# Attention and a gated layer in one kernel: the seven-product layer of two token blocks begun one tile sooner, less attention work between half-width steps, one fetch sooner

## The chip, the cores and the metric

The kernel runs on one core of a Trainium2 chip. The metric is the device time of one execution in microseconds (us), the median of three runs of the same program. TensorE (PE in the rows) multiplies matrices into PSUM banks, VectorE (DVE) and ScalarE (ACT) work element by element and empty the banks, GpSimd (POOL) does element work between SBUF tiles, SyncE (SP) issues DMAs. Each engine runs its own queue strictly in order.

## The reference

```python
def _attn_ref(q, k, v):               # (8, 8, 576, 64): batch, heads, sequence, head size
    # chunks of 64 along the sequence: S = Q K^T / 8 within a chunk
    scores = scores - np.max(scores, axis=-1, keepdims=True)
    attn = np.exp(scores)
    attn = attn / (np.sum(attn, axis=-1, keepdims=True) + 1e-09)
    out = np.matmul(attn, v_c)
def _moe_ref(x, w_gate, w_val, w_out):  # x: 4608 x 512, widths 512 -> 1536 -> 512
    gate = 1.0 / (1.0 + np.exp(-(x @ w_gate)))
    return (gate * (x @ w_val) @ w_out)
```

The attention's output is reordered to 4608 tokens of 512 numbers and goes through the gated layer. All is float32.

## The kernel before, in words

The 4608 tokens are nine blocks of 512, the hidden width is twelve slices f of 128. A float32 product is made of three passes over rounded halves (high and low part of each operand), so an operand is first *split*: ScalarE casts the high part, VectorE subtracts it to get the low part. Block 0 is worked plainly at the start. Blocks 1 and 2 share one hidden tile per slice (`hidden_kept`, line 297): for each block and slice TensorE makes a gate tile and a value tile (12 matmuls each, line 278), ScalarE takes the sigmoid (line 303), VectorE multiplies (line 305). A gate-and-value pair is called a tile step here; it takes two of the four `acc` banks. The first four slices of block 1 are done in two half-width parts a and b (256 tokens); the part b steps stand in `LEAD`.

The product with `w_out` is done for two blocks at once by a seven-product scheme (`down_begin`, `down_products`): 42 *small steps* q of 12 matmuls each (line 661), every one with its own split (lines 636 and 637). `down_begin` issues the first two weight loads and the splits of q = 0, 1 and 2; in `down_products` the split of q + 3 is issued just before the matmuls of q. The pairs of blocks 3 to 8 then use the same scheme for the first product too (`first`, `middle`, `last`, line 504).

The attention of later blocks is woven in. `flow` yields it piece by piece: score products on TensorE (line 173) into two `psa` banks, two VectorE transposes out of them (738), a maximum (742) whose 32-partition halves are exchanged by four ScalarE copies (721), a subtraction (746, 747), an exponential (749, which needs another function table than the sigmoid, so a table load stands ahead of each change), the value products of the unit before (244) into the same two banks and their copies out (264 and 265, or 261), a sum (765), exchanged again, the division (769, 772, 773) and two transposes (777). A number that `flow` yields is a price in credit; `tick(share)` grants credit, so `SHARES` sets how much is issued after each step. "S" and "A" are places where TensorE's products may be inserted. After the last unit of a pair, `operands` makes the seven operands of the pair's first product: a difference on VectorE (481), a cast on ScalarE (485), the low part on VectorE (494).

The order written is the order issued on TensorE, VectorE, SyncE and GpSimd, and on ScalarE as far as blocks 1 and 2 are concerned. GpSimd meanwhile forms sums of weight quarters, writes them to DRAM, and fetches the next quarters (`keep_sums`, `fetch`); the first fetch for the pairs' second half is issued by SyncE (line 376).

Of the kernel before, what the change touches and what calls it, by code (L numbers as in the profile page):

```python
# [19 lines left out]
NF = 12  # L20
# [29 lines left out]
SHARES = {1: 1.4, 2: 1.3, "up": 1.0, "turned": 0.36}  # L50
# [3 lines left out]
def chunk_attn_moe(ctx: ExitStack, tc: tile.TileContext, q, k, v, w, out, turned_out):  # L54
# [288 lines left out]
    def keep_given(p, which):  # L343

        if p < RESIDENT:
            t = given[p, which] = dp.tile([P, 3, 2, 256], F32, name=f"given{p}{which}")
            for n, (f, k) in enumerate(((2 * p, 0), (2 * p, 1), (2 * p + 1, 1))):
                nc.sync.dma_start(t[:, n], wt[f, which][:, :, k * 256:(k + 1) * 256].bitcast(F32))
        else:
            t = whole[p, which] = dp.tile([P, 2, 2, 4, P], F32, name=f"whole{p}{which}")  # L350
            for n in range(2):
                src = wt[2 * p + n, which].bitcast(F32).rearrange("p a (k m) -> p (a k) m", k=2)
                for c in range(2):
                    nc.sync.dma_start(t[:, n, c], src[:, :, c * P:(c + 1) * P])
# [240 lines left out]
    def down_sums(n, f):  # L595

        if n < 0:
            if f in (0, 4, 6):
                t = wp.tile([P, 4, TB], F32, tag=f"u{f // 2 - f // 4}", name="t12")
                for e in range(4):  # L600
                    k = e + (0, 4, 8)[f // 2 - f // 4]
                    (t1 if k < 6 else t2)[k % 6] = t[:, e]
        elif f == 0:
            t = xp.tile([P, 8, TB], F32, tag="x", name="t1")
            for e in range(8):
                t1[e] = t[:, e]
        elif f == 6:
            both = sb.tile([P, 4, TB], F32, tag="a_both", name="t2")
            t2.update({0: t1[6], 1: t1[7], **{2 + e: both[:, e] for e in range(4)}})
        e = f % 6  # L610
        b11, b12 = (hid[n, e][:, b] for b in range(2))
        if f < 6:
            nc.vector.tensor_tensor(out=t1[e], in0=b12, in1=b11, op=ALU.subtract)
        else:
            b22 = hid[n, f][:, 1]
            nc.vector.tensor_tensor(out=t2[e], in0=b22, in1=t1[e], op=ALU.subtract)
            nc.vector.tensor_tensor(out=b12, in0=b22, in1=b12, op=ALU.subtract)
# [22 lines left out]
    def down_begin(n):  # L640

        ring["splits"], *ring["weights"] = rotation
        rotation[:] = rotation[4:] + rotation[1:4] + rotation[:1]
        for i in range(2):
            load_down(n, i)
        for q in range(3 if n < LAST else 6):
            down_split(n, q)
# [136 lines left out]
    def advance():  # L784
        now["unit"] += 2 * (now["item"] == "A")
        now["item"] = next(ahead, None)
        now["since"] = now["ticks"]

    def tick(share):
        now["ticks"] += 1  # L790
        now["credit"] += share
        while now["item"] is not None:
            if isinstance(now["item"], float):
                if now["credit"] < now["item"] / 2:
                    return
                now["credit"] -= now["item"]
            elif not (now["item"] == "wait" and now["ticks"] > now["since"] + 1
                      or now["item"] == "next" and now["ticks"] > now["since"]
                      or now["item"][0] in ("open", "freed") and now["item"][1] <= now[now["item"][0]]):
                break  # L800
            advance()
        now["credit"] = min(now["credit"], share)

    def insert(upto=4 * NB, pieces=0):


        if now["item"] == "S" or (
                now["item"] == "A" and now["unit"] < upto and now["ticks"] >= now["since"] + pieces):
            advance()

    def due(n):

        while now["item"] is not None and len([x for x in xc if x[0] == n]) < 7:
            advance()
# [4 lines left out]
    def step(m, f, span, aside=False):  # L819
        if m:  # L820
            hidden_kept(m, f, spans[span], aside)
        else:
            pending.append(hidden(m, f, spans[span]))
# [4 lines left out]
    def run(op):  # L828
        what, arg = op[0], op[1:]
        if what == "L":  # L830
            load(int(arg))
        elif what == "V":
            load_values(int(arg))
        elif what in "Ss":
            scores(int(arg), what == "s")
        elif what == "E":
            softmax(int(arg))
        elif what in "Tt":
            transposes(int(arg), what == "t")
        elif what == "A":  # L840
            values(int(arg), pairs.pop(int(arg) // 2)["pt"])
        elif what == "W":
            load_weights(int(arg[:-1]), arg[-1])
        elif what == "C":
            f, part = arg.split(".")
            convert_weights(int(f), int(part))
        elif what == "G":
            for which in range(2):
                keep_given(int(arg), which)
        elif what == "K":  # L850
            keep_outer(int(arg))
        elif what == "H":
            m, f = arg.split(".")
            step(int(m), int(f.rstrip("ab")), f.lstrip("0123456789"))
        else:
            finish()
# [5 lines left out]
    def keep(n=1):  # L862
        for _ in range(n):
            if kept:
                keep_sums(*kept.pop(0))
# [5 lines left out]
    def singles():  # L871
        for op in LEAD.split():
            run(op)
            if op[0] == "H":
                tick(SHARES[1])
                insert(12, 1)
        for m in range(1, FIRST_PAIR):
            upto = 4 * (m + 2) if m == 1 else 4 * (m + 3)
            while now["unit"] < 4 * (m + 1):
                advance()  # L880
            for f in range(FIRST_STEP if m == 1 else 0, NF):
                if m == 2 and f == 7:
                    now["open"] = 0
                if m == 2 and f == NF - 1:
                    down_begin(-1)
                step(m, f, "", True)
                tick(SHARES[m])
                insert(upto, 1)
                if m == 2 and f < NF - 2:
                    down_sums(-1, f)  # L890
                tick(SHARES[m])
                insert(upto, 1)
                if givens:
                    keep_given(*givens.pop(0))
                if kept[0][2] is None:
                    keep()

    def pair(n):
        m0 = FIRST_PAIR + 2 * n
        upto = 4 * (m0 + 4)  # L900
        order = [(p, which) for p in range(6) for which in range(2)]
        if n >= 0:
            due(n)
        for i, (p, which) in enumerate(order if n >= 0 else ()):
            if i + 1 < len(order) and i > 0:
                load_group(n, *order[i + 1])
            first(n, p, which)
            tick(SHARES["up"])
            if i:
                keep(2)  # L910
                last(n, *order[i - 1])
                tick(SHARES["up"] if i < 11 else 0)
                insert(upto, 1)
                if i > 1:
                    down_sums(n, i - 2)
            middle(n, p, which)
            tick(SHARES["up"] if i < 11 else 0)
            insert(upto, 1)
        if n >= 0:
            down_begin(n)  # L920
            last(n, *order[-1])
        now["open"] = n + 1

        def between(q):
            now["freed"] = q if n < 0 else 99
            if n < LAST:
                if q in (32, 36):
                    load_group(n + 1, 0, 0, ((q - 32) // 4,))
                if n < 0 and q == 32:
                    fetch(*kept[0], nc.sync)  # L930
                tick(SHARES["turned"] if q > 3 else 0)
                insert(upto, 1)

        down_products(n, between)
        if n < LAST:
            load_group(n + 1, 0, 1)
# [42 lines left out]
```

## Time and profile before

| | |
|---|---|
| median of 3 runs | 906.49 us (904.53 to 906.89) |
| the profiled execution | 904.59 us, span 902.8 us |
| TensorE busy | 869.1 us, 96% of the span |
| VectorE, ScalarE, GpSimd busy | 674.6, 397.4, 244.4 us |
| DMA | 216.53 MB, 240 GB/s on average |

The span runs from the first to the last instruction of the core. The first 60 us bring in weights and hold most of TensorE's idle time. Blocks 1 and 2 lie from about 169 to 298 us, their seven-product layer from 298 to 360 us, and the three pairs of blocks follow. In a row of the timeline, the first number is the start, the second the length of the stretch, and what stands in square brackets is the idle time just before it and who ended it.

### The profile page before, as it was taken

The numbers are of one execution on the slowest core, as the hardware profiler recorded it, in microseconds if no ns is written. First come the engines' busy times: TensorE is split into PE (matmuls) and PEld (weight loads), VectorE is DVE, ScalarE is ACT, GpSimd is POOL, SyncE is SP. The second block draws the span as 40 slices with busy tenths as digits, with TensorE's granted clock in tenths as the row PEclk, the third lists the DMA queues.
The fourth block names the chain that finished last, engine by engine and source line by source line (L and its number), as shares of the span: only waits on it lengthen the run. The fifth ranks groups of instructions, "written<-read, shape, count | busy, mean of one in ns | idle before, by whom it ended". The sixth has DMA issues, their size and how long they took to land.

```text
span 902.8 us, 15594 instructions
## 1 busy us (share of the span) xinstructions
PE 869.1 (96%) x6016; PEld 711.7 (79%) x6016; DVE 674.6 (75%) x1007; ACT 397.4 (44%) x734; POOL 244.4 (27%) x275
## 2 busy tenths in 40 slices
PE   4799999999999899999999999999999999999998
PEld 3678879888877687887887888888878888888886
DVE  6998955476878778787987895877778945555973
ACT  6988743334444644234326551442345511122540
POOL 0111217999994002888940000000000000000000
PEclk7999999999999999999999999999999999999999
DMA  8885586599775666999986678595565785564772
GB/s 314 292 268 197 162 282 234 204 332 374 262 252 184 210 203 234 362 328 360 351 290 196 200 237 271 194 298 168 187 190 181 225 280 198 181 202 154 232 211 94
DMA packets 152107, 216.53 MB, mean 240 GB/s; under 512 B 9056, under 2 KB 90464, under 8 KB 150496
## 3 DMA queue, kind: packets, MB, share of 16 engines
q1 hardware_dynamic: 143248, 178.29, 61.2%
q0 software_dynamic: 8784, 37.23, 11.0%
q8 instruction: 48, 0.79, 0.3%
q14 instruction: 27, 0.22, 0.1%
HBM read 169.87 MB, written 45.61 MB: 239 GB/s over the span
## 4 chain that ended last, share of the span: by engine, by line
PE 63%; DMA 1%; DVE 1%; ACT 1%; issue 1%; SPq 0%; ACTq 0%; DVEq 0%
PE dx L661 17%; PE cy L504 16%; PE cz L504 11%; PE cx L504 10%; PE dz L661 7%; DMA wr<-sums 1%; PE av L244 1%; PE sc L173 1%; DVE hx L637 0%; ACT hx L636 0%; SPq L144 0%; DVE raw L481 0%; ACT xc L485 0%; DVE hid L685 0%; ACT hs L636 0%
## 5 line engine op out<-in xcount | busy, mean ns | idle before, releaser
L504 PE MATMUL cy<-xc,wr 128*128 128x512 f32 x648 | 159.4, 390 | 1.8 <-DMA wr<-sums 1.8
L504 PEld LDWEIGHTS cy<-xc,wr 128*128 128x128 f32 x648 | 121.3, 188 | 28.2 <-DVE mx L742 2.2
L278 PE MATMUL acc<-xt,w 128*128 128x512 f32 x480 | 112.6, 392 | 0.0
L504 PE MATMUL cz<-xc,wr 128*128 128x512 f32 x432 | 107.2, 392 | 0.0
L504 PE MATMUL cx<-xc,wr 128*128 128x512 f32 x432 | 106.0, 391 | 0.0
L661 PE MATMUL dx<-hs,wd 128*128 128x512 f32 x432 | 102.1, 390 | 2.9 <-ACT hs L636 2.7
L278 PEld LDWEIGHTS acc<-xt,w 128*128 128x128 f32 x480 | 89.1, 188 | 18.9
L278 PE MATMUL g<-xt,w 128*128 128x256 f32 (+1 forms) x528 | 94.7, 335 | 7.0 <-ACT hf L287 2.6
L661 PEld LDWEIGHTS dx<-hs,wd 128*128 128x128 f32 x432 | 81.0, 188 | 20.5 <-ACT hs L636 3.1
L278 PEld LDWEIGHTS g<-xt,w 128*128 128x128 f32 x528 | 80.0, 190 | 18.9 <-ACT hf L287 3.7
L504 PEld LDWEIGHTS cx<-xc,wr 128*128 128x128 f32 x432 | 80.6, 188 | 17.3 <-DMA wr<-given 0.4
L504 PEld LDWEIGHTS cz<-xc,wr 128*128 128x128 f32 x432 | 80.3, 188 | 16.9
L661 PE MATMUL dx<-hx,wd 128*128 128x512 f32 x288 | 71.1, 393 | 1.1 <-DVE hx L637 0.7
L661 PEld LDWEIGHTS dx<-hx,wd 128*128 128x128 f32 x288 | 53.7, 188 | 14.6 <-DVE hx L637 2.2
L522 DVE TENSOR_TENSOR s<-cy,s 128x512 f32<-128x512 f32 x36 | 24.9, 690 | 51.4 <-PE cy L504 44.8
L520 ACT COPY s<-cx 128x512 f32<-128x512 f32 x36 | 21.2, 589 | 83.8 <-PE cx L504 83.7
L636 ACT CAST hs<-hid 128x512 fp32r<-128x512 f32 x66 | 38.3, 620 | 43.7 <-PE dx L661 26.5
L637 DVE TENSOR_TENSOR hs<-hid,hs 128x512 fp32r<-128x512 f32 x66 | 43.6, 703 | 13.8 <-ACT hs L636 13.8
L661 PE MATMUL dz<-hs,wd 128*128 128x512 f32 x216 | 51.2, 389 | 0.0
L359 POOL DMA_DIRECT2D outer<-w x24 | 18.8, 782 | 117.2 <-issue 49.0
L544 ACT ACTIVATE hid<-cx 128x512 f32<-128x512 f32 x18 | 10.8, 598 | 83.3 <-PE cx L504 83.3
L661 PEld LDWEIGHTS dz<-hs,wd 128*128 128x128 f32 x216 | 40.5, 188 | 8.4
(135 smaller groups left out, 1424.0 us busy)
## 6 DMA issues: line engine op xcount, KB each, us to landing
wr<-sums SPq DMA_DIRECT2D x72, 512.0 KB, 6.1
w_raw<-w_in SPq DMA_DIRECT2D x36, 512.0 KB, 5.3
wd<-outer SPq DMA_DIRECT2D x72, 256.0 KB, 5.3
wd<-outer_sums SPq DMA_DIRECT2D x16, 1024.0 KB, 6.1
wr<-whole SPq DMA_DIRECT2D x54, 256.0 KB, 4.4
qt<-q_in SPq DMA_DIRECT2D x36, 256.0 KB, 4.6
kt<-k_in SPq DMA_DIRECT2D x36, 256.0 KB, 5.0
vt<-v_in SPq DMA_DIRECT2D x36, 256.0 KB, 4.4
```

The source lines that it names most:

```text
L173: nc.tensor.matmul(sc[i][half * D:(half + 1) * D, n0:n0 + D], lhsT=x[rows, a, chunk], rhs=y[rows, a, chunk], start=True, stop=True)
L244: nc.tensor.matmul(av[c][a * D:(a + 1) * D, n0:n0 + D], lhsT=vt[u][rows, i, a, t, :], rhs=pt[rows, i, u, t, a, :], start=True, stop=True)
L278: nc.tensor.matmul(ps[:, tok], lhsT=wt[f, which][:, wpart, c:c + P], rhs=xt[m][:, part, 2 * u + i, tok], start=n == 0, stop=n == 11)
L359: nc.gpsimd.dma_start(outer[:, f, c], src[:, :, c])
L504: nc.tensor.matmul(bank, lhsT=lhs(wpart, c), rhs=x[:, part, c], start=start and k == 0, stop=stop and k == 5, skip_group_check=True)
L520: nc.scalar.copy(s1, x)
L522: nc.vector.tensor_tensor(out=u2, in0=y, in1=s1, op=ALU.add)
L544: nc.scalar.activation(hid[n, f][:, 0], x, AF.Sigmoid)
L636: nc.scalar.copy(hi, src)
L637: nc.vector.tensor_tensor(out=lo, in0=src, in1=hi.bitcast(F32), op=ALU.subtract)
L661: nc.tensor.matmul(bank[to][c], lhsT=down_lhs(r, f, wpart, c), rhs=down_in[q][part], start=r in (1, 6, 5) and (f, i) == (0, 0), stop=stop ...
```

## The change

Three numbers differ. In `singles`, a step in `LEAD` (half width) grants 1.0 of credit to the attention instead of 1.4. `down_begin` for blocks 1 and 2 is called ahead of the tile step of slice 10 of block 2 instead of slice 11. SyncE's fetch for GpSimd is issued after small step 28 instead of 32.

```diff
             if op[0] == "H":
-                tick(SHARES[1])
+                tick(SHARES["up"])
                 insert(12, 1)
...
-                if m == 2 and f == NF - 1:
+                if m == 2 and f == NF - 2:
                     down_begin(-1)
                 step(m, f, "", True)
...
-                if n < 0 and q == 32:
+                if n < 0 and q == 28:
                     fetch(*kept[0], nc.sync)
```

Since credit moves on from step to step, the first number shifts the attention of blocks 1 and 2 against the tile steps throughout. On ScalarE, at the half-width steps of slices 2 and 3, the order before was as follows (`g` is a gate product at half width, `mx` and `other` belong to the attention's maximum, `acc` is a full tile):

```order
L303 ACTIVATE hid<-g_1829 128x256
L721 COPY other<-mx_1859 32x32 x4
L303 ACTIVATE hid<-g_1866 128x256
L749 ACT_TABLE_LOAD
L749 ACTIVATE pr<-pr 128x1024
L303 ACT_TABLE_LOAD
L303 ACTIVATE hid<-g_1897 128x256
```

It is now:

```order
L303 ACTIVATE hid<-g_1829 128x256
L303 ACTIVATE hid<-g_1859 128x256
L721 COPY other<-mx_1887 32x32 x4
L303 ACTIVATE hid<-g_1894 128x256
L749 ACT_TABLE_LOAD
L749 ACTIVATE pr<-pr 128x1024
L303 ACT_TABLE_LOAD
```

The sigmoid of slice 2 has moved ahead of the exchange, that of slice 3 ahead of the exponential. On VectorE the first full tiles and the division of the same unit stood so before (`hid<-acc` is the product of a tile step, `sums` belongs to the division, `pt` to its transposes, `sc` is the next unit's score bank):

```order
L305 TENSOR_TENSOR hid<-acc,hid 128x512
L765 TENSOR_REDUCE sums_1954<-pr 128x32
L769 SCALAR_TENSOR_TENSOR sums_1954<-sums_1954,other 128x32
L772 RECIPROCAL sums_1954<-sums_1954 128x32
L773 TENSOR_TENSOR pr<-pr,sums_1954 128x1024
L777 STREAM_TRANSPOSE pt<-pr 128x512 x2
L305 TENSOR_TENSOR hid<-acc,hid 128x512
L738 STREAM_TRANSPOSE pr<-sc 128x512 x2
L742 TENSOR_REDUCE mx_2058<-pr 128x32
L305 TENSOR_TENSOR hid<-acc,hid 128x512
L746 TENSOR_TENSOR mx_2058<-mx_2058,other 128x32
```

And now:

```order
L305 TENSOR_TENSOR hid<-acc,hid 128x512
L765 TENSOR_REDUCE sums_1954<-pr 128x32
L305 TENSOR_TENSOR hid<-acc,hid 128x512
L769 SCALAR_TENSOR_TENSOR sums_1954<-sums_1954,other 128x32
L772 RECIPROCAL sums_1954<-sums_1954 128x32
L773 TENSOR_TENSOR pr<-pr,sums_1954 128x1024
L777 STREAM_TRANSPOSE pt<-pr 128x512 x2
L738 STREAM_TRANSPOSE pr<-sc 128x512 x2
L305 TENSOR_TENSOR hid<-acc,hid 128x512
L742 TENSOR_REDUCE mx_2104<-pr 128x32
L746 TENSOR_TENSOR mx_2104<-mx_2104,other 128x32
```

The product of the tile step now stands between the sum and the division, and no longer between the maximum and its use. This order comes back in every later unit of blocks 1 and 2. On TensorE the score products and the value products stand one tile step later.

At the end of block 2, ScalarE had this order (`hs` and `hx` are splits of the seven-product layer, `raw` the last value products' copies, `xc` the operands of the next pair):

```order
L749 ACTIVATE pr<-pr 128x1024
L261 COPY raw<-av 128x4x2x64 x2
L303 ACT_TABLE_LOAD
L303 ACTIVATE hid<-acc 128x512
L485 CAST xc<-raw 128x1024 x3
L636 CAST hs<-hid 128x512 x2
L636 CAST hx<-hid 128x512
L303 ACTIVATE hid<-acc 128x512
L485 CAST xc<-raw 128x1024
L636 CAST hx<-hid 128x512
```

It is now:

```order
L749 ACTIVATE pr<-pr 128x1024
L636 CAST hs<-hid 128x512 x2
L636 CAST hx<-hid 128x512
L303 ACT_TABLE_LOAD
L303 ACTIVATE hid<-acc 128x512
L261 COPY raw<-av 128x4x2x64 x2
L485 CAST xc<-raw 128x1024 x3
L303 ACTIVATE hid<-acc 128x512
L485 CAST xc<-raw 128x1024
L636 CAST hx<-hid 128x512
```

The first three splits have moved ahead of the last values' copies and of the operand casts; the fourth split still comes behind the fourth operand cast. On SyncE the fetch into `again` has moved ahead of one pair of stores, one load of layer weights and the two loads of the next pair's first group, right behind the weight load of small step 28.

## Rows read from the trace of the kernel before

**Rows 1.** The stretch of blocks 1 and 2 in the view of busy times by stretch: start and end, length, busy time and number of instructions by engine, TensorE's clock, DMA share, GB/s.

```profile
150.00:300.00 150.00, 143.40 (x1496) 118.75 (x1496) 104.91 (x119) 59.87 (x115) 121.37 (x113) 1.00 0.80 273
```

**Rows 2.** The waits of TensorE over the whole span: who waited for whom, us in total, times, longest.

```profile
PE dx L661 <- ACT hs L636: 2.7, 1, 2.7
PE cy L504 <- DMA wr<-sums: 1.8, 1, 1.8
PE g L278 <- ACT hid L303: 1.5, 1, 1.5
...
PE sc L173 <- ACT raw L261: 1.4, 3, 1.1
```

**Rows 3.** Timeline of TensorE at the half-width steps, and at the end of block 2 and the start of its seven-product layer.

```profile
165.92 3.14 PE L278 MATMUL g<-xt,w 128*128 128x256 f32 x24 [1.52 <-ACT hid L303]
168.90 5.63 PE L278 MATMUL acc<-xt,w 128*128 128x512 f32 x24
...
286.47 11.17 PE L278 MATMUL acc<-xt,w 128*128 128x512 f32 x48
300.35 0.49 PE L661 MATMUL dx<-hs,wd 128*128 128x512 f32 x1 [2.71 <-ACT hs L636]
```

**Rows 4.** Timeline of ScalarE at the half-width steps.

```profile
164.56 0.89 ACT L721 COPY other<-mx 32x32 f32<-32x32 f32 x4 [4.06 <-DVE mx L742]
165.48 0.38 ACT L303 ACTIVATE hid<-g 128x256 f32<-128x256 f32 x1
```

**Rows 5.** Timeline of VectorE at the first full tiles: the start of the division of one unit, the product behind it, the transposes of the next.

```profile
177.46 0.68 DVE L769 SCALAR_TENSOR_TENSOR sums<-sums,other 128x32 f32<-128x32 f32 x1 [1.02 <-ACT other L721]
...
181.73 0.69 DVE L305 TENSOR_TENSOR hid<-acc,hid 128x512 f32<-128x512 f32 x1 [0.42 <-issue]
182.34 1.30 DVE L738 STREAM_TRANSPOSE pr<-sc 128x512 f32<-128x512 f32 x2
```

**Rows 6.** Timeline of VectorE in block 2, two units: the products that waited for ScalarE, and one division.

```profile
246.75 0.69 DVE L305 TENSOR_TENSOR hid<-acc,hid 128x512 f32<-128x512 f32 x1 [1.64 <-ACT hid L303]
253.84 0.69 DVE L305 TENSOR_TENSOR hid<-acc,hid 128x512 f32<-128x512 f32 x1 [2.84 <-ACT hid L303]
267.69 0.69 DVE L305 TENSOR_TENSOR hid<-acc,hid 128x512 f32<-128x512 f32 x1 [1.64 <-ACT hid L303]
273.74 0.69 DVE L305 TENSOR_TENSOR hid<-acc,hid 128x512 f32<-128x512 f32 x1 [0.61 <-ACT hid L303]
278.08 2.38 DVE L769 SCALAR_TENSOR_TENSOR sums<-sums,other 128x32 f32<-128x32 f32 x1
```

**Rows 7.** Timeline of ScalarE from the last exponential of block 2's stretch to the fourth split.

```profile
291.27 1.06 ACT L749 ACTIVATE pr<-pr 128x1024 f32<-128x1024 f32 x1 [0.81 <-DVE pr L747]
292.23 1.05 ACT L261 COPY raw<-av 128x512 f32<-128x512 f32 x2
293.30 1.28 ACT L303 ACT_TABLE_LOAD   x1
294.60 0.60 ACT L303 ACTIVATE hid<-acc 128x512 f32<-128x512 f32 x1
295.09 1.99 ACT L485 CAST xc<-raw 128x1024 fp32r<-128x1024 f32 x2
...
299.68 1.13 ACT L636 CAST hs<-hid 128x512 fp32r<-128x512 f32 x2
...
304.94 0.62 ACT L636 CAST hx<-hid 128x512 fp32r<-128x512 f32 x1
```

**Rows 8.** Timeline of VectorE there: the first low part of an operand, and the first difference.

```profile
296.17 1.23 DVE L494 TENSOR_TENSOR xc<-raw,xc 128x1024 fp32r<-128x1024 f32 x1 [0.24 <-ACT xc L485]
297.43 1.22 DVE L481 TENSOR_TENSOR raw<-raw 128x1024 f32<-128x1024 f32 x1
```

**Rows 9.** Groups of VectorE's instructions by line and shape: busy us, mean ns of one, idle before. The first two rows are of the stretch 176 to 280 us, the third of 494 to 640 us.

```profile
L305 DVE TENSOR_TENSOR hid<-acc,hid 128x512 f32<-128x512 f32 x15 | 10.2, 681 | 15.8 <-ACT hid L303 13.4 <-PE acc L278 1.9 <-issue 0.4
L617 DVE TENSOR_TENSOR hid<-hid 128x512 f32<-128x512 f32 x2 | 3.3, 1638 | 0.0
...
L617 DVE TENSOR_TENSOR hid<-hid 128x512 f32<-128x512 f32 x3 | 2.0, 683 | 0.0
```

**Rows 10.** Timeline of SyncE (the weight load of small step 28, and the fetch) and of GpSimd (the first instruction that needs the fetched tile).

```profile
335.05 1.25 SPq L586 DMA_DIRECT2D wd<-outer_sums  x1
...
347.76 0.62 SPq L376 DMA_DIRECT2D again<-whole  x1
...
355.64 2.17 POOL L420 TENSOR_TENSOR a_both<-again 128x256 f32<-128x256 f32 x2 [23.09 <-DMA again<-whole]
```

**Rows 11.** Timeline of VectorE (splits of small steps 36 to 41 around the start of GpSimd's work) and of TensorE at small step 39.

```profile
349.31 1.29 DVE L637 TENSOR_TENSOR hs<-hid,hs 128x512 fp32r<-128x512 f32 x2 [0.61 <-ACT hs L636]
...
355.38 0.69 DVE L637 TENSOR_TENSOR hx<-hid,hx 128x512 fp32r<-128x512 f32 x1 [1.69 <-ACT hx L636]
355.99 2.37 DVE L637 TENSOR_TENSOR hs<-hid,hs 128x512 fp32r<-128x512 f32 x2
...
356.13 1.41 PE L661 MATMUL dz<-hx,wd 128*128 128x512 f32 x5 [0.23 <-DVE hx L637]
```

## The prediction

> **What bounds the kernel now.** I read the busy times first. TensorE is busy 96% of the span, and what it lacks lies mostly in the first 60 us, which the change leaves alone. In the stretch of blocks 1 and 2 it is busy 143.4 of 150 us [rows 1], so some 6.6 us are to be had there. The view of waits names them [rows 2]: 1.5 us once for a sigmoid at the half-width steps, 1.4 us in three pieces where score products wait for ScalarE to empty the banks, and 2.7 us at the first small step of the seven-product layer, which waits for its split. Elsewhere only the 1.8 us on a weight load stands out.
>
> Then I asked who is late. TensorE may run ahead of VectorE by two tile steps, since a step takes two of four banks. In block 2 VectorE's products of the tile steps wait for ScalarE, not for TensorE: 1.64 and 2.84 us, then 1.64 and 0.61 us [rows 6]. So from there on it is the chain between VectorE and ScalarE, which hand work to and fro, that ends last; TensorE meets it at the banks and at the splits. That makes the question: when does that chain bring the fourth split, at 305.56 us before (304.94 + 0.62) [rows 7]? Behind it no small step waits until the 0.23 us at 356.13 [rows 11].
>
> **The half-width steps.** Before, the sigmoid of slice 2 stood behind four copies that begin at 164.56, and TensorE lost 1.52 us up to 165.92 [rows 3, 4]. In the new order it stands ahead of them, and those 1.52 us go. The first full tile starts at 168.90 - 1.52 = 167.4. This shortens the whole only if TensorE's arrival sets the end of the stretch. By the step above it doesn't, so it counts zero in the sum and comes back in a rival.
>
> **What the shifted order does to the chain.** First unit: before, the division ran from 177.46 to 181.31 (181.73 less 0.42 idle), 3.85 us, then the product, then the transposes at 182.34 [rows 5]. Now the product of the second full tile stands ahead of the division. That tile ends at 167.4 + 11.2 for two tile steps [rows 3], at 178.6; product 0.69, division 3.85, a handoff of 0.1: the transposes start at 183.2, 0.85 later than before, with the same work done.
>
> Later units: the waits inside one unit change places. After the sum, the next product needs the copies and a sigmoid on ScalarE: 0.90 + 0.60 [rows 4, 7], with 0.15 for the handoffs 1.65 us, nothing of VectorE's between. After the subtraction it needs exponential, table load and sigmoid: 1.06 + 1.28 + 0.60 [rows 7], with handoffs 3.1 us, again with nothing between, because the differences for the seven products (lines 613, 616 and 617) now stand ahead of the subtraction, where they cover the copies. Together 4.75 us. Before, the same places cost 1.64 + 2.84 = 4.48 in the one unit, and 1.64 + 0.61 = 2.25 in the other [rows 6], where two long differences lay beneath the exponential. So the first kind gains nothing and loses 0.25, the second loses 2.5. Of that some 2.2 come back: the division of that unit, whose first instruction took 2.38 us beside GpSimd at 278.08 [rows 6], slips past the end of GpSimd's work. I take +0.3 for this unit and +0.2 for each of the four others, 1.1 in all.
>
> Line 617, two SBUF inputs, takes 1638 ns while GpSimd works and 683 ns where it doesn't (the page's slices show it idle there); line 305, with one input from PSUM, takes 681 beside GpSimd [rows 9]. The Trainium skill (GPSIMD Engine Reference, Specifications) says that GpSimd shares its SBUF interfaces with VectorE, with contention for instructions with two SBUF inputs. The trace agrees on who is slowed, not that each one is: by the rule all five such instructions on the path of small step 39 (below) would pay, and the sum would be 912.4 instead of 910.7; by the rows a part of them does.
>
> **Beginning the layer one tile sooner.** The first three splits now follow the exponential at once; those of q = 1 and 2 are ready in time. The fourth is not moved: it still stands behind the fourth operand cast, and that cast behind the last value products, which are now one tile step later. From the end of the exponential (292.33) to 305.56 it took 13.23 us before [rows 7]. Now, in order: three splits 1.75, table 1.28, sigmoid 0.60, two copies 1.05, first cast 1.00 [rows 7]; on VectorE the low part 1.23 and the difference 1.22 [rows 8]; third cast 1.00, sigmoid 0.60, product 0.69, low part 1.23, difference 1.22, fourth cast 1.00, split 0.62. Sum 14.5, so +1.3. TensorE then waits little at the first small step and 5 to 6 us at the fourth. The move by itself is worth nothing.
>
> Another rule would make it worse. The table load takes 1.28 us and the sigmoid begins 1.30 after it [rows 7]. The Trainium skill (ScalarE: Activation LUTs, What ACT_TABLE_LOAD costs) adds a drain of about 1.38 us to every switch. With it five units and the end would each cost up to 1.4 more, some 8 us; the rows show no such gap, so I leave it out.
>
> The chain so brings the fourth split 0.85 + 1.1 + 1.3 = 3.25 us later, and all behind it follows. Bounds: how GpSimd's instructions meet VectorE's is chance, and the nearest row is 1638 against 683 ns, 0.95 for one instruction [rows 9]. If two of them meet it less, and the first unit loses nothing, the term is 3.25 - 1.9 - 0.85 = 0.5; if the 2.2 don't come back it is 5.5. I take 3.25, since each piece is nearest to its own row.
>
> **The fetch.** SyncE issued it at 347.76, and GpSimd began at 355.64, 7.9 us later. Now it follows the weight load that ends at 336.3 [rows 10], 11.5 us sooner; the queue it passes holds one pair of stores and three loads, each 0.6 us later at most, which are needed later than that. So GpSimd begins near the small steps 30 to 32 instead of 41, and works while VectorE makes the last splits. There the chain has no room: step 39 waited 0.23 us already [rows 11]. From 349.31 to 356.07 its path holds five instructions with two SBUF inputs (two splits, one, a difference, one). The two splits at 355.99 took 2.37 us beside GpSimd, the two at 349.31 took 1.29 without [rows 11]: 0.54 each. All five: +2.7. At the other end GpSimd finishes 11 us sooner, where nothing waited for it; but the weight load that cost 1.8 us [rows 2] shares the DMA queues with its traffic and may be spared: -1.8. Between the ends I take +0.95, as if two of five met it and nothing else changed.
>
> **Sum.** 3.25 + 0.95 = 4.2 us on the profiled execution's own 904.59, so 908.8. That execution is 1.9 below the median of the runs, 906.49; I put the same 4.2 on the median: 910.7.
>
> **Rivals.** *TensorE sets the pace after all.* If the chain keeps up, in units no longer than the three tile steps and their inserts, TensorE gets back 1.5 at the half-width steps, 1.4 at the banks and most of 2.7 at the layer's start: 906.5 - 5.6 = 900.9. For it: score and value products come one tile step later, when the banks are empty. Against it: VectorE already waits for ScalarE, not for TensorE, in four places of four [rows 6]. It decides where the fourth split would come before TensorE's last tile plus three small steps.
>
> *It cancels.* Contention falls well (0.5), the fetch costs nothing or saves its 1.8: 905.2 to 907.0, no change. For it: the size of the chance in rows 9. Against it: the 1.3 at the end hang on no contention.
>
> *GpSimd hits harder.* The full 2.7 and a first term of 5.5: 906.5 + 8.2 = 914.7. For it: step 39 has no slack. Against it: GpSimd spends part of its time in casts and DMA issues.
>
> **How the numbers follow.** A measurement of this kernel can tell 0.3%, 2.7 us, from no change. My forecast (907.5 to 913) gets 0.52, TensorE's pace 0.15, cancelling 0.26, the harder hit 0.07. Of the forecast's 0.52 about 0.13 lies below 909.2. Faster: 0.13 of the first rival and 0.02 of the second, 0.15. Same: 0.13 + 0.02 + 0.22 = 0.37. Slower: 0.39 + 0.02 + 0.07 = 0.48. The range is 904.0 to 914.0: above it lies half of the harder hit, below it most of the first rival.
>
> **What would show it.** The wait of 1.52 us gone, and the first full tile at about 167.4. The last value products without a wait. The wait at the first small step under 2 us, and one of 4 to 7 us at the fourth (`hx`, line 636); its second matmul near 309.5. GpSimd's first sum near small step 31, and a wait of 0.5 to 3 us at step 39. I am wrong if the fourth split comes before 305.5, if GpSimd's two-input neighbours stay near 0.69 us, or if TensorE's wait is at a place not named.

## The result, and the profile after

| | before | changed |
|---|---|---|
| median, 5 runs each on one chip | 906.89 us (904.53 to 907.1) | 913.02 us (910.95 to 915.46) |
| ratio, 95% interval | | 1.0082 (1.0068 to 1.0096) |
| the profiled execution, its span | 904.59 us, 902.8 us | 915.46 us, 913.7 us |
| TensorE busy | 869.1 us | 875.0 us |

The change makes the kernel slower by 0.82%, some 7.4 us; the medians lie 6.1 apart. The forecast was 910.7 in a range of 904.0 to 914.0.

The two profiled executions differ by more, 10.9 us. To say where, I need a mark in both that lies ahead of the work the change reorders. The first score products among the half-width steps serve. Here they are in the timeline of TensorE before, with the products behind the wait of 2.71 us at the first small step [rows 3], and the first `dz` product of the layer, small step 24:

```profile
157.29 1.16 PE L173 MATMUL sc<-qt,kt 64*64 64x64 f32 x64
...
301.07 2.79 PE L661 MATMUL dx<-hs,wd 128*128 128x512 f32 x11 [0.23 <-DVE hs L637]
...
334.85 2.88 PE L661 MATMUL dz<-hs,wd 128*128 128x512 f32 x12
```

And here in that of the changed kernel, with all that TensorE later waits for in blocks 1 and 2 and their layer:

```profile
163.17 1.16 PE L173 MATMUL sc<-qt,kt 64*64 64x64 f32 x64
164.26 8.90 PE L278 MATMUL g<-xt,w 128*128 128x256 f32 x72
173.00 3.36 PE L278 MATMUL acc<-xt,w 128*128 128x512 f32 x14
...
282.29 2.47 PE L173 MATMUL sc<-qt,kt 64*64 64x64 f32 x64 [3.43 <-ACT raw L261]
284.69 12.71 PE L278 MATMUL acc<-xt,w 128*128 128x512 f32 x48
...
306.87 1.52 PE L661 MATMUL dx<-hx,wd 128*128 128x512 f32 x6
314.57 3.23 PE L661 MATMUL dx<-hx,wd 128*128 128x512 f32 x6 [6.18 <-ACT hx L636]
317.60 3.42 PE L661 MATMUL dx<-hs,wd 128*128 128x512 f32 x12
...
345.34 2.88 PE L661 MATMUL dz<-hs,wd 128*128 128x512 f32 x12
...
367.36 0.49 PE L661 MATMUL dz<-hx,wd 128*128 128x512 f32 x1 [1.47 <-ACT hx L636]
368.44 1.45 PE L661 MATMUL dz<-hx,wd 128*128 128x512 f32 x5 [0.58 <-DVE hx L637]
```

This execution reached the mark 5.9 us later, though nothing ahead of the mark is reordered. Some 3.2 us of it are a wait of 1.93 us of value products for a load (line 244, waits below; 0.26 before) and slower products behind it (the 64 value products took 1.84 us for 1.16, the next 48 products 6.84 for 6.02); the rest lies further ahead. Profiles of six kernels have such a wait of 1.8 to 1.9 there, two of them of kernels with before's order at this place; the other nine have 0.4 at most. What decides it I don't know, so I count from the mark on, or from the first full tile.

The wait of 1.52 us [rows 3] is gone: the full tiles start 9.83 us behind the mark instead of 11.61. The wait for the fourth split, 6.18 us, is new. Behind it stands something I hadn't listed: the six matmuls of this small step take 3.23 us, and those of the step ahead of it 1.52. (A small step has six matmuls; the twelve given above are two steps, which one row often joins.) The view of busy times by stretch (columns as in [rows 1]) shows a mean granted clock of 0.66 there, between the two levels of 1.2 and 2.4 GHz, where before had 1.00:

```profile
314.00:321.00 7.00, 6.43 (x19) 4.94 (x20) 6.21 (x10) 2.70 (x5) 0.00 (x0) 0.66 0.28 79
```

The view of TensorE's waits over the whole span (us in total, times, longest; compare [rows 2]):

```profile
PE dx L661 <- ACT hx L636: 6.2, 1, 6.2
...
PE sc L173 <- ACT raw L261: 3.4, 1, 3.4
...
PE av L244 <- DMA vt<-v_in: 1.9, 1, 1.9
...
PE cx L504 <- DMA wr<-given: 1.0, 1, 1.0
```

The chain that brings this split, on ScalarE (compare [rows 7]), from the last exponential on:

```profile
299.41 1.06 ACT L749 ACTIVATE pr<-pr 128x1024 f32<-128x1024 f32 x1 [0.31 <-DVE pr L747]
300.37 1.12 ACT L636 CAST hs<-hid 128x512 fp32r<-128x512 f32 x2
...
312.95 1.04 ACT L485 CAST xc<-raw 128x1024 fp32r<-128x1024 f32 x1 [3.02 <-DVE raw L481]
313.91 0.61 ACT L636 CAST hx<-hid 128x512 fp32r<-128x512 f32 x1
```

And on VectorE (compare [rows 5, 6]): the first unit, and the products that wait.

```profile
184.16 0.69 DVE L305 TENSOR_TENSOR hid<-acc,hid 128x512 f32<-128x512 f32 x1 [3.52 <-issue]
184.77 0.18 DVE L769 SCALAR_TENSOR_TENSOR sums<-sums,other 128x32 f32<-128x32 f32 x1
...
188.37 1.31 DVE L738 STREAM_TRANSPOSE pr<-sc 128x512 f32<-128x512 f32 x2
...
257.95 0.69 DVE L305 TENSOR_TENSOR hid<-acc,hid 128x512 f32<-128x512 f32 x1 [3.04 <-ACT hid L303]
...
262.49 0.69 DVE L305 TENSOR_TENSOR hid<-acc,hid 128x512 f32<-128x512 f32 x1 [1.64 <-ACT hid L303]
```

For the later units, VectorE alone, from the transposes that end the first unit to the start of the last exponential (length, busy time and number of instructions, clock, DMA share, GB/s), before:

```profile
182.34:291.27 108.93, 85.31 (x94) 1.00 0.82 280
```

and changed:

```profile
188.37:299.41 111.04, 81.28 (x94) 0.97 0.83 283
```

The fourth split is there at 314.52, 151.35 behind the mark; before it was 148.27. So it comes 3.08 us later. From there to the first `dz` product TensorE takes 30.82 us, before 29.29: 1.53 more. The last two waits, at small step 39, add 2.05 us where before there was 0.23 [rows 11], and the way from the first `dz` to the first pair becomes 1.88 us longer; behind that 1.47 are won back. From the mark to the end of the span this pair of executions differs by 5.0 us (750.5 and 745.5).

### The profile page after: what moved, and what is told of

Read it like the earlier page. It is cut to its first block, busy times and chain, and to the rows that moved or that the text cites. A ratio compares the mean times of both kernels' runs of the same rounds, so it can differ in the third digit from the quotient of the medians.

```text
span 913.7 us, 15576 instructions
## 1 busy us (share of the span) xinstructions
PE 875.0 (96%) x6016; PEld 717.9 (79%) x6016; DVE 673.3 (74%) x1007; ACT 397.6 (44%) x734; POOL 243.1 (27%) x275
## 4 chain that ended last, share of the span: by engine, by line
PE 74%; ACT 9%; DVE 9%; DMA 5%; issue 2%; SPq 0%; ACTq 0%; DVEq 0%
PE dx L661 17%; PE cy L504 16%; PE cz L504 11%; PE cx L504 11%; PE acc L278 7%; PE dz L661 7%; DMA w_raw<-w_in 3%; PE g L278 3%; PE sc L173 2%; PE av L244 2%; ACT w_raw L125 1%; ACT w_raw L124 1%; DMA wr<-given 1%; ACT w L131 1%; DVE pr L747 1%
```

## The experiments

Ratios are against before on the same chip, with the 95% interval. 0.1% is 0.9 us.

**The three numbers apart.** Less attention at the half-width steps alone:

```diff
-                tick(SHARES[1])
+                tick(SHARES["up"])
```

> Only the credit of the half-width steps. Theory (the order on VectorE and ScalarE delays the fourth split of the layer): the whole of the 3 us and the clock's loss come with this edit alone, so +3 to +6 us against before, with the wait now mostly at the first small step (5 to 7 us) since the layer isn't begun sooner. Rival (the early start of the layer pushes sigmoid and operand casts back): this edit alone is within 1 us of before or 1 to 2 us faster, by the 1.5 us saved at the half-width steps.

910.66 us, 1.0058 (1.0038 to 1.0079). Alone it costs 5.3 us. In its trace the first small step waits 4.1 us for its split, in place of 2.71 [rows 3], the 11 matmuls behind that take 4.23 us for 2.79, and the fourth split is there 152.09 us behind the mark, 3.8 later than before.

The early begin alone:

```diff
-                if m == 2 and f == NF - 1:
+                if m == 2 and f == NF - 2:
                     down_begin(-1)
```

> Only the layer begun one tile step sooner. Theory: worth nothing, -1 to +1 us, since the fourth split stays behind the fourth operand cast; the wait moves from the first small step (2.7 us before) to the fourth (3 to 5 us). If one longer wait drops TensorE's clock, up to +2. Rival (early start pushes things back): +3 us or more.

905.84 us, 1.0012 (0.9998 to 1.0026): no difference. The wait of 2.71 us at the first small step goes, and one of 3.58 comes at the fourth. In its trace the fourth split comes 1.04 us sooner (147.23 behind the mark), but the 18 matmuls behind it take 3.23 and 4.03 us, and from the split to the first `dz` it is 31.42 us for 29.29. So here a gain and a larger loss all but cancel.

The early fetch alone:

```diff
-                if n < 0 and q == 32:
+                if n < 0 and q == 28:
                     fetch(*kept[0], nc.sync)
```

> Only the fetch at small step 28. Theory: the wait at small step 39 grows from 0.23 to about 2 us, of which 0 to 1.5 come back at the loads of the first pair, so +0.5 to +2 us. Rival (the fetch costs nothing, GpSimd's sooner end pays): -1.8 to 0.

911.1 us, 1.0064 (1.0047 to 1.0082). Alone it costs as much as the first number, and more than the 2 us I had expected at most. In its trace small step 39 waits 2.35 us, 12 matmuls behind that take 4.48 us, and the first pair waits 2.45 for a weight load. It also has something that the fetch can't have made, since it lies ahead of it: behind a wait of 2.66 us at the first small step, where before waits 2.71, the products are slower.

```profile
301.03 4.22 PE L661 MATMUL dx<-hs,wd 128*128 128x512 f32 x11 [0.22 <-DVE hs L637]
```

The first two numbers together, the fetch left at 32:

```diff
-                if n < 0 and q == 28:
+                if n < 0 and q == 32:
                     fetch(*kept[0], nc.sync)
```

> The changed kernel with the fetch back at small step 32. Theory: the wait of 6 us at the fourth split and the half clock behind it stay, the wait at small step 39 is under 0.5 us: +4 to +5.5 us against before, 1 to 2 less than the changed kernel's +6.1. Rival (the fetch costs nothing): +6 or more.

910.41 us, 1.0062 (1.0042 to 1.0083). So in the changed kernel 5.6 us belong to the late fourth split and what follows from it, and 1.8 to the fetch, a difference that the intervals alone don't settle. Effects don't add up: alone the pieces cost 5.3, 1.1 and 5.8.

**The operand casts out of the way.** My explanation says that the fourth split is late because it stands behind the four casts of operands. Then letting these begin later should take the waits away, whatever the begin:

```diff
-                if m == 2 and f == 7:
-                    now["open"] = 0
```

Without these two lines the operands are opened behind `down_begin` (line 922). With before and the early begin:

> The kernel before with the layer begun one tile step sooner, and the next pair's operands (lines 481, 485, 494) opened only when the layer's small steps start, not in slice 7 of block 2. Theory (the fourth split is late because it stands behind four operand casts): the splits come before the casts, no wait at the first four small steps, -3 to -4 us against before. Rival (the last values' copies and sigmoids set the fourth split, not the casts): a wait of 2 us or more stays, -1 to 0.

901.55 us, 0.9955 (0.9939 to 0.997). With before alone:

> The kernel before with nothing but the operands opened late. Theory: as with the layer begun sooner, -3 to -4 us, since that edit is worth nothing. Rival: begun sooner is worth something once the casts are out of the way: 1 us or more behind e5_begin_open_late.

901.51 us, 0.9964 (0.9949 to 0.9978). Both are faster than both kernels, and again the begin is worth nothing. On ScalarE of the second the fourth split now stands ahead of the casts:

```profile
297.45 0.60 ACT L303 ACTIVATE hid<-acc 128x512 f32<-128x512 f32 x1
297.94 0.61 ACT L636 CAST hx<-hid 128x512 fp32r<-128x512 f32 x1
298.44 2.01 ACT L485 CAST xc<-raw 128x1024 fp32r<-128x1024 f32 x2
```

and TensorE goes from the last tile into the layer with no wait:

```profile
287.27 11.22 PE L278 MATMUL acc<-xt,w 128*128 128x512 f32 x48
298.32 2.88 PE L661 MATMUL dx<-hs,wd 128*128 128x512 f32 x12
301.04 2.88 PE L661 MATMUL dx<-hx,wd 128*128 128x512 f32 x12
```

The same two lines taken out of the changed kernel:

> The changed kernel with the operands opened late in the same way. Theory: the wait of 6.2 us at the fourth split and the 2.2 us of half clock behind it go; what is left against before is the fetch: -2 to +1 us. Rival (the order on VectorE and ScalarE has cost the time upstream of the layer, in the clock): +3 us or more.

907.99 us (902.07 to 912.47), 1.0023 (0.9999 to 1.0046). And out of the kernel with the first two numbers, fetch at 32:

> The changed kernel with the fetch back at small step 32 and the operands opened late. Theory: the 1.5 us at the half-width steps now count, TensorE's arrival sets the layer: -3 to -6 us against before, the best of the four; the wait of 3.4 us for the bank in block 2 may take 1 to 2 of it with its half clock. Rival (the shifted order is bad by itself): no better than e7_open_late.

902.99 us (901.26 to 904.23), 0.9964 (0.9951 to 0.9977). With the casts out of the way the shifted order costs nothing: 0.9964 with it and without it. The early fetch does, some 5 us, against the 1 at most that I had expected, and it brings a scatter of 10 us where there were 3.

**What of the fetch costs.** Late operands and the early fetch, on before:

```diff
-                if m == 2 and f == 7:
-                    now["open"] = 0
...
-                if n < 0 and q == 32:
+                if n < 0 and q == 28:
```

> The kernel before with its operands opened late, and the early fetch beside it. My theory: with no other wait left in these stages, the fetch still costs, because GpSimd's sums then meet VectorE's splits of small steps 36 to 41 and the work of the first pair: a wait of 1 to 2.5 us at small step 39, half clock behind it, in all 2 to 6 us above the late opening alone (901.5), so 903.5 to 907.5. Rival: the fetch cost only because other waits were there; then it is harmless here, and the time stays at 901 to 903.

908.25 us (902.67 to 911.55), 1.0023 (1.0004 to 1.0042): 5.3 above the 0.9964 without the fetch. Then the same, with GpSimd held until VectorE has made the low part of the operand of the pair's second product:

```diff
+                if n == 0 and i == 1:
+                    held = sm.tile([P, 1], F32, name="held", bufs=1)
+                    nc.gpsimd.tensor_copy(held, xc[0, "T2"][:, 1, 0, :1].bitcast(F32))
```

> As the run before, but GpSimd's work is held back by one small copy that reads an operand VectorE makes after the last splits (near 358 to 360 us), so that only the transfer comes early. My theory: it is GpSimd's element work beside VectorE that costs; held back it costs nothing, and the time is that of the late opening alone, 901 to 903, with no wait at small step 39. Rival: the early transfer itself costs, through the DMA queues; then the time stays with the run before (903.5 to 907.5).

903.35 us (900.58 to 906.64), 0.9977 (0.9961 to 0.9992). 4.2 of the 5.3 are gone. (The trace of the early one is of an execution of 911.4 us, slower than its median; that of the held one took the median.) SyncE's transfer is as early as in the run before (it is issued at 336.52); what is held is GpSimd's element work, and two transfers that GpSimd itself issues. The groups of VectorE's instructions from 340 to 362 us by line and shape, early:

```profile
L637 DVE TENSOR_TENSOR hs<-hid,hs 128x512 fp32r<-128x512 f32 x4 | 3.8, 982 | 0.0
...
L637 DVE TENSOR_TENSOR hx<-hid,hx 128x512 fp32r<-128x512 f32 x2 | 2.5, 1235 | 1.7 <-ACT hx L636 1.7
...
L685 DVE TENSOR_TENSOR hid<-dx,hid 128x512 f32<-128x512 f32 x2 | 1.3, 676 | 0.0
```

and held:

```profile
L637 DVE TENSOR_TENSOR hs<-hid,hs 128x512 fp32r<-128x512 f32 x4 | 2.6, 688 | 0.6 <-ACT hs L636 0.6
...
L637 DVE TENSOR_TENSOR hx<-hid,hx 128x512 fp32r<-128x512 f32 x2 | 1.4, 693 | 1.8 <-ACT hx L636 1.7
L685 DVE TENSOR_TENSOR hid<-dx,hid 128x512 f32<-128x512 f32 x2 | 1.3, 684 | 0.0
```

The splits, with two inputs in SBUF, take 982 and 1235 ns in the mean beside GpSimd and 690 without; the sum out of a PSUM bank (685) takes the same in both. One pair shows how, GpSimd's instruction and the split beside it, in the early run:

```profile
351.19 1.61 POOL L386 TENSOR_TENSOR a_both<-a_both 128x512 fp32r<-128x512 f32 x1
```

```profile
351.57 1.78 DVE L637 TENSOR_TENSOR hx<-hid,hx 128x512 fp32r<-128x512 f32 x1
```

From GpSimd's end at 352.80 the split took 0.55 us more, nearly the 0.69 of a split that nothing holds up. The Trainium skill (SBUF — State Buffer, SBUF: two separate sides) says that the pair of ports which the two engines share is an exclusive lock, held for a whole instruction, and that whoever comes second blocks: this pair agrees with it.

TensorE pays at small step 39, and again behind it. Early:

```profile
357.60 0.56 PE L661 MATMUL dz<-hx,wd 128*128 128x512 f32 x1 [2.33 <-ACT hx L636]
358.33 2.50 PE L661 MATMUL dz<-hx,wd 128*128 128x512 f32 x5 [0.17 <-DVE hx L637]
360.63 3.21 PE L661 MATMUL dz<-hs,wd 128*128 128x512 f32 x12
...
372.72 1.66 PE L504 MATMUL cx<-xc,wr 128*128 128x512 f32 x6 [2.08 <-DMA wr<-given]
375.35 3.02 PE L504 MATMUL cy<-xc,wr 128*128 128x512 f32 x12 [0.97 <-DMA wr<-sums]
```

Held:

```profile
356.16 1.43 PE L661 MATMUL dz<-hx,wd 128*128 128x512 f32 x5 [0.23 <-DVE hx L637]
357.43 2.89 PE L661 MATMUL dz<-hs,wd 128*128 128x512 f32 x12
...
369.02 3.02 PE L504 MATMUL cy<-xc,wr 128*128 128x512 f32 x12 [0.23 <-DMA wr<-sums]
```

So with late operands most of the early fetch's price is GpSimd's early work: beside VectorE's last splits it brings the wait and half clock behind it, and with it come waits for the first pair's weights. Whether these loads are late because of GpSimd's own transfers or because SyncE issues them behind late stores, I didn't try.

The same hold in the changed kernel:

> The changed kernel with the same hold on GpSimd. My theory: the two waits at small step 39 (1.47 and 0.58 us) go, and the time is that of the changed kernel without the early fetch, 1 to 2.5 us below the changed kernel, some 5 to 6 above before. Rival, the transfer costs: as the changed kernel, 6 to 8 above before.

912.65 us, 1.0078 (1.0057 to 1.0099): no gain, a miss. The waits at step 39 do go (0.23 us is left), but the first pair then waits 1.32 and 0.71 us for its weights. Against the changed kernel's trace, 1.66 us are won between the mark and the first pair, and 1.43 are lost behind it. Why the loss moves here, and not with late operands, is open.

**The clock.** TensorE kept busy in place of the wait at the fourth split, in the changed kernel:

```diff
+            if n < 0 and q == 3:
+                idle = ps_g.tile([P, TB], F32, tag="g0", name="idle", bufs=1)
+                for _ in range(24):
+                    nc.tensor.matmul(
+                        idle, lhsT=down_lhs(1, 0, 0, 0), rhs=down_in[0][0], start=True, stop=True,
+                        skip_group_check=True)
```

> The changed kernel with 24 extra products ahead of small step 3, whose result nobody reads: TensorE is busy in place of most of the 6.18 us in which it waits for the fourth split. My theory: the granted clock stays full behind that wait, the matmuls of small steps 3 and 4 take 1.5 and 2.9 us instead of 3.2 and 3.4, and the time is 1.5 to 2.5 us below the changed kernel, less what the products themselves reach beyond the split. Rival: half clock behind the wait is no loss, since VectorE and ScalarE set the pace there too; then the time is that of the changed kernel, 6 to 8 above before.

912.05 us, 1.0079 (1.0051 to 1.0106): the time of the rival. In its trace, though, the clock is back, and the layer from its start to the first `dz` is 1.8 us shorter (39.57 for 41.34), as I expected; then step 39 waits 2.04 us and its last matmuls run at half clock, and a load makes the first pair wait 2.31. In this trace what was won was lost again at the next gate, the fetch. So the same filling in the kernel without the early fetch:

> The 24 extra products ahead of small step 3 in the kernel with the two shifts but the fetch at its old place (910.4, 5.6 above before), so that no wait at small step 39 can take back what is gained. My theory: the 5.6 are 3.3 of a late fourth split and some 2 of half clock behind the wait; with the wait filled the matmuls behind it run at full clock and the time is 1.5 to 2.5 below, 3 to 4.5 above before. Rival: half clock costs nothing, because the splits of VectorE and ScalarE set the pace there too; then the time stays at 5 to 6.5 above before.

907.68 us, 1.0031 (1.0015 to 1.0047), against 1.0062 without the filling. Here 2.8 us by the ratios stay won. Two rows of the view of busy times by stretch (after the bar of GpSimd: clock, DMA share, GB/s), without the filling:

```profile
300.00:325.00 25.00, 19.14 (x74) 14.99 (x73) 15.86 (x21) 13.34 (x22) 0.00 (x0) 0.86 0.46 144
```

and with it:

```profile
300.00:325.00 25.00, 24.16 (x105) 19.45 (x104) 17.30 (x24) 15.36 (x25) 0.00 (x0) 1.00 0.51 161
```

The matmuls behind the split, without it:

```profile
311.58 3.23 PE L661 MATMUL dx<-hx,wd 128*128 128x512 f32 x6 [5.86 <-ACT hx L636]
314.61 3.90 PE L661 MATMUL dx<-hs,wd 128*128 128x512 f32 x12
```

and with it:

```profile
313.73 0.51 PE L661 MATMUL dx<-hx,wd 128*128 128x512 f32 x1 [0.61 <-ACT hx L636]
314.46 1.44 PE L661 MATMUL dx<-hx,wd 128*128 128x512 f32 x5 [0.22 <-DVE hx L637]
315.73 2.89 PE L661 MATMUL dx<-hs,wd 128*128 128x512 f32 x12
```

The intervals of the two ratios overlap a little; that the clock is what differs rests on these rows, and on the way from the end of the fourth split to the first `dz`, in which it doesn't matter how late the split is. It takes 29.24 and 29.26 us in the two filled kernels, as in before (29.29), and 30.82, 30.84 and 31.30 in the changed kernel, the held one and the one with the fetch at 32. So by the traces half clock costs 1.5 to 2.0 us here. (The filled kernel's profiled execution, 911.02 us, is above its median: ahead of the mark it waited 1.82 us for a load.)

## Why the prediction was right and wrong

It forecast slower, which was the right direction, and too little: 4.2 us where 7.4 were measured. By the ratios the 7.4 are 2.8 of a late fourth split (the filled run without the early fetch), 2.8 of half clock behind it (the same run unfilled less the filled one) and 1.8 of the fetch (the changed kernel less the one with the fetch at 32). Each has an uncertainty of 1.5 to 2.5 us. The traces give 3.1 for the first, 1.5 to 2.0 for the second and 1.8 at small step 39 for the third.

**The term of the chain, 3.25 us: right in size, in part by luck.** The fourth split came 3.08 us later, and 3.05 to 3.67 in the four other kernels with the first two numbers. Its pieces were less right than their sum. The first unit lost 0.15 and not 0.85 (transposes at 25.20 behind the mark, before 25.05): its product began 0.3 sooner than I had put it, and the division with its transposes took 3.5 us instead of 3.85. The later units lost 2.1, twice the 1.1, since the last exponential ended 137.30 us behind the mark, and 135.04 before. Here both sides of the account were too small. The new waits were nearly as I had sized them, 3.04 and 1.64 us against 3.1 and 1.65, and the unit of the two long differences waits 2.4 us longer, as forecast; but the four others wait 0.5 to 1.7 us longer, where I had 0.2. In all VectorE stood idle 29.8 us of this stretch instead of 23.6, 6.1 more. What came back was more too: its 94 instructions were busy 81.28 us instead of 85.31, 4.0 less, and the division of 2.38 us took 0.18, as forecast. From the last exponential to the split it was 0.8 (14.05 less 13.23) and not 1.3.

**What was missing: half clock behind a wait.** I wrote that a wait of 4 to 7 us would stand at the fourth split, found it, and counted as its price only how late the split is. The step that failed is "and all behind it follows": what follows does so at 1.2 GHz at first (granted clock 0.50 from 314.5 to 317.6 us). The next 18 matmuls take 3.23 and 3.42 us, at full clock 1.52 and 2.88. Against before, where the first of these steps also waited 0.22 for its low part, that makes 1.53 us up to the first `dz`; when TensorE is kept busy, 2.8 come back by the ratio and 1.6 to 2.0 by the traces. Before could hardly show the price: its longest wait here, 2.71 us [rows 3], is followed by 11 matmuls in 2.79 us, and the clock is 1.00 [rows 1]; only the first of the page's forty slices shows a lower clock, and there TensorE is idle for the most part. I could have asked what a longer wait does.

**The early begin, nothing by itself: right in size.** 1.0012 alone, and 901.55 against 901.51 with late operands. The reason given, that the fourth split stands behind the fourth cast, is shown by the runs with late operands: without it there is no wait, and 3.3 to 4.1 us are won. Alone, though, the begin brought the split 1.04 us sooner and lost 2.1 to half clock behind a longer wait (its trace), so that near zero is in part luck.

**The half-width steps, zero: right.** The 1.52 us went, and nothing of it reached the end, in the changed kernel or with late operands. In the traces of the latter the layer began 141.43 us behind the mark with the shifted order and 140.00 without: the new wait of score products (below) took more than was won.

**The fetch, 0.95 us: mis-sized, within its bounds in this kernel, beyond them alone.** GpSimd's sums began 8.95 us behind the fetch's issue, not 7.9, at step 31 or 32 as forecast (8.5 us ahead of step 38, with 1.36 us to a step). They met the splits that I had named, and TensorE lost 2.05 us less 0.23 there, inside the 2.7 I had as the worst case. In the changed kernel that is most of it: 1.8 by ratio. But alone it costs 5.8, and with late operands 5.3, and there the bound fails: I had priced one wait, and not half clock behind it and late loads behind that. Why it costs less in the changed kernel the runs don't show; in the trace of the filled one, without half clock behind the fourth split, the fetch took back what had been won. The saving of 1.8 us on the weight load is not shown to be the fetch's: 0.99 us of such a wait are left in the changed kernel, for 1.8 [rows 2], but with the fetch at 32 such waits in the first pair come to anything from none to 1.8 us in the eight traces (none in the filled kernel, 1.76 with late operands alone).

**The rivals.** TensorE did not set the pace: the fourth split came later and TensorE waited for it. The change did not cancel: the split was late by 3.05 us or more in all five kernels with both shifts. GpSimd did cost more than I took, 1.8 by ratio for 0.95, but the 914.7 of that rival rests on a first term of 5.5, and the chain came 3.08 late. The wait of score products, 3.43 us at 282.29, I had not named at all, and a wait at a place not named was one of my signs of being wrong. The score products and the tiles behind it also run slower (2.47 us for 1.16, 12.71 for 11.18). In the changed kernel it lies ahead of the split, and TensorE waits at the split regardless; the kernel with late operands that has it too (3.79 us) is as fast by ratio as the one without.

## What to carry to other kernels

Starting a stage earlier helps only if the *last* of its inputs comes earlier: find the instruction that is not moved and see what stands ahead of it on its engine; here taking out the two lines that opened the four casts early was worth 3.3 us, and moving the begin nothing. Price a new wait of several microseconds on TensorE with the slow stretch behind it, not with its length alone. Work that is moved earlier on an engine off the critical path is not free if it shares something with an engine that has no slack there; hold it and see.

## What the runs showed that I had not expected

- Waits of 2.04 to 2.35 us at step 39 were followed by half clock: 12 matmuls in 3.2 to 4.5 us instead of 2.88. Behind 1.47 and 0.58 us in the changed kernel, and behind 2.08 us at a weight load (row at 372.72), they ran at full clock. The clearest pair is before and the kernel with the early fetch alone, whose instructions are the same up to that point: at the first small step they wait 2.71 and 2.66 us, and the next 11 matmuls take 2.79 and 4.22 us. So the length of one wait alone doesn't tell it, and the same stretch can pay for it in one execution and not in another.
- Prices don't add up: the fetch costs 5.8 us alone, 1.8 in the changed kernel, and 4.3 where the wait at the fourth split is filled (1.0079 against 1.0031), with an uncertainty of 1.6, 2.2 and 2.9 us. It may be that a wait costs less when another stands ahead of it; that is not shown.
- The kernels with the early fetch and late operands scatter over 9 to 10 us (902.07 to 912.47, 902.67 to 911.55), the ones without it, or with it held, over 2.8 to 6.1. I take it that how GpSimd's instructions meet VectorE's differs from execution to execution, and with it the price; with one trace of each kernel this is not shown.
